# Gathering the third expert's rows right behind the second expert's, before the first scatter

## The chip, the core and the metric

The kernel runs on one core of a Trainium2 chip. The metric is the device time of one execution in microseconds (us). A profiled execution gives the trace, from which all single durations below come. The engines are named as in the profile: PE (matmuls), PEld (its weight loads), DVE, ACT, POOL and SP; SP and POOL mostly issue transfers.

## What is computed

The reference is an attention block whose output is the input of a mixture of experts:

```python
kv  = einsum('bhsd,bhse->bhde', k, v)           # batch 8, heads 8, seq 576, head_dim 64
out = einsum('bhsd,bhde->bhse', q, kv)
x   = out / sqrt(mean(out*out, -1) + 1e-6) * g_norm     # then reshaped to 4608 rows of 512

do_compute = x @ w_skip > 0                      # the other rows are returned as they are
e   = argmax(x @ w_gate)                         # one of 8 experts for each row
y   = softmax(x @ w_gate)[e] * (relu(x @ w1[e]) @ w2[e])   # w1: 512x1024, w2: 1024x512
out = x + y
```

## The kernel before

The attention part writes the rows of x to `out` in HBM and keeps the gate's logits. From these it works out, on the core, which rows go to which expert. The experts are sorted by their number of rows, so "expert 0" is the one with the most. Each has a fixed room for its rows (`ROOMS`: 352, 352, 320, 288, 288, 288, 256 and 256 rows, cut into pieces of 128, 64 and 32 rows by `PIECES`).

The rows of an expert are fetched from `out` with indirect DMAs issued by POOL, one for each piece (`gather_piece`, line L1084). They land in a tile `xg`; expert 0 has one of its own (`xg0`), the others share a pool of three (`gather_all`, L1376). PE transposes them (`expert_in`, L1093), layer 1 and layer 2 follow, DVE multiplies by the gate's value and adds x (`result`, L1336), and POOL scatters the rows back to `out` with an indirect DMA (L1339). Scatters are declared independent of each other, since each row has one slot. Gathers and scatters touch the same tensor `out`, so a gather behind a scatter in program order waits for its landing, and a scatter behind a gather likewise.

The order of instructions is written out by hand. Each engine takes its own in the order of the program text. In the stretch that matters here this is:

- Rows of expert 0 beyond the first 192, then those of expert 1, are gathered (L1500; six indirect DMAs on POOL, 134.9 to 142.4 us). The first 192 rows of expert 0 were gathered earlier (L863) and are already in the layers.
- Layer 2 for these first rows ends, layer 1 for the rest of expert 0 follows (L1112), and beside it the gate's values are placed (`first_tables`, L1405).
- The first 192 rows are scattered (`result` at L1407 and L1413, two indirect DMAs on POOL, at 154.07 and 155.40 us). Rows of expert 1 are transposed and its weight sums are begun on DVE (L1414).
- The rows of expert 2 are gathered (L1423, three indirect DMAs: two pieces of 128 rows and one of 64).
- Layer 2 for the rest of expert 0 (L1427, recorded at L1124): a piece of 128 rows, and one of 32 rows in matmuls with 32 columns, in two halves each. Then its results and scatters (L1430).
- Experts 1 to 7 follow, each in a form with 7 products in place of 8 (`fast_1`, `fast_2`; the matmuls are recorded at L1192, ACT's copies of partial sums at L1202, DVE's additions at L1196, its sums of weights at L1134 and L1140). At its beginning expert r gathers the rows of expert r + 2 (L1390).

The weights of an expert are 2 MB for each layer. SP loads them (L336 and L346) into two sets of tiles in turn, as soon as PE has read the set's former contents. The loads of expert 1 are issued at 142.0 and 142.7 us.

A second use of the same code, `experts(whole, ...)` at L1552, serves a loop that runs only when an expert has more rows than its room. It passes `yps0 = None`.

Of the kernel before, what the change touches and what calls it, by code (L numbers as in the profile page):

```python
# [17 lines left out]
def kernel(  # L18
# [213 lines left out]
    for a in range(2):  # L232
        r = slice(a * 64, (a + 1) * 64)
# [45 lines left out]
    for r, cap in enumerate(ROOMS):  # L279
        pieces, off = [], 0  # L280
# [710 lines left out]
    with tc.tile_pool(name="wpool_b", bufs=1, reuse_waits="tile") as wpool_b, \  # L991
# [89 lines left out]
        def gather_piece(xg, piece, src, asrc):  # L1081
            off, m, col, aside = piece
            idx = asrc if aside else src
            nc.gpsimd.indirect_dma_start(  # L1084
                out=x_of(xg, off, m), out_offset=None, in_=cut_rows(m)[:, :],
                in_offset=bass.IndirectOffsetOnAxis(ap=idx[:, col:col + 1], axis=0))

        def expert_in(xg, xt, piece):
            off, m = piece[0:2]
            x = x_of(xg, off, m)  # L1090
            xp = bank()[:, :].rearrange("p (j t) -> p j t", t=P)
            for j in range(DC * m // P):
                last = nc.tensor.transpose(out=xp[:, j, :], in_=x[:, j * P:(j + 1) * P],  # L1093
                                           identity=ident[:, :])
            turned(xt, xp, off, m)
            return last

        def new_xt():
            return ffn.tile([P, DC, CAP], FP32, tag="xt", name="xt")
# [8 lines left out]
        def layer_1(r, xt, ht, cols, fs):  # L1108
            for f in fs:
                hps = bank()  # L1110
                for dc in range(DC):
                    nc.tensor.matmul(out=hps[:, cols], lhsT=w_sb[r][0][:, dc, f * P:(f + 1) * P],  # L1112
                                     rhs=xt[:, dc, cols], start=(dc == 0), stop=(dc == DC - 1))
                nc.scalar.activation(out=ht[:, f, cols], in_=hps[:, cols], func=ACT.Relu)
# [69 lines left out]
        def do(work, n=None):  # L1184
            n = len(work) if n is None else min(n, len(work))
            for job in work[:n]:
                job()
            del work[:n]
# [141 lines left out]
        def result(piece, yps, xg, tables, group):  # L1330

            off, m, col, aside = piece
            n = DM * m // P
            rows, gate = tables[1 if aside else 0]
            x = x_of(xg, off, m)
            nc.vector.scalar_tensor_tensor(  # L1336
                out=x, in0=yps[:, 0:n], scalar=gate[:, col:col + 1], in1=x,
                op0=ALU.mult, op1=ALU.add)
            ins = nc.gpsimd.indirect_dma_start(  # L1339
                out=cut_rows(m)[:, :],  # L1340
                out_offset=bass.IndirectOffsetOnAxis(ap=rows[:, col:col + 1], axis=0),
                in_=x, in_offset=None, bounds_check=N * P // m - 1, oob_is_err=False)
            tc.declare_no_dep(ins.ins, group=group, reason="each row has one slot")
            tc.add_to_no_dep_group(group, ins.ins)
# [24 lines left out]
        def load_ahead(r, behind=None):  # L1369
            for ahead in (r, r + 1):  # L1370
                if ahead < E and ahead not in w_sb:
                    load_weights(ahead, wpool_b if ahead % 2 else wpool_a, behind)
# [3 lines left out]
        def gather_all(r, pieces, src, asrc):  # L1376
            if r < E:
                xgs[r] = xg0 if r == 0 else gather_pool.tile([P, CK, DM], FP32, tag="xg", name="xg",
                                                             bufs=3)
                for piece in pieces[r]:  # L1380
                    gather_piece(xgs[r], piece, src, asrc)

        def experts(pieces, widths, srcs, xt, ht, yps0, tables, group):

            for r in range(E):
                load_ahead(r)
                if yps0 is not None and r == E - 1:
                    nc.gpsimd.drain()
                if r:
                    gather_all(r + 2, pieces, *srcs)  # L1390
                todo = pieces[r]
                end = widths[r]
                new = {}

                def enter(some):
                    for piece in some:
                        expert_in(xgs[r + 1], new["xt"], piece)

                more = pieces[r + 1] if r + 1 < E else []
                if more:  # L1400
                    new["xt"] = new_xt()
                beside = []
                if r == 0:
                    if yps0 is not None:
                        tables = first_tables(lambda fs: layer_1(r, xt, ht, slice(KEPT, end), fs),  # L1405
                                              tables)
                        result(first[0], yps0[0], xgs[0], tables, group)  # L1407
                    else:
                        layer_1(r, xt, ht, slice(0, end), range(FC))
                    enter(more[0:1])  # L1410
                    if yps0 is not None:
                        tables = again_gates(tables)
                        result(first[1], yps0[1], xgs[0], tables, group)  # L1413
                    do(w1_sums(r + 1))  # L1414
                    enter(more[1:])
                else:
                    fast_1(r, xt, ht, end // 2, w2_sums(r), lambda: enter(more[0:1]))
                    enter(more[1:])
                if more:
                    n = widths[r + 1] // 2  # L1420
                    beside = x_sums(r + 1, new["xt"], n) + (w1_sums(r + 1) if r else [])
                if r == 0:
                    gather_all(2, pieces, *srcs)  # L1423
                    ys = [bank() for _ in todo]
                    for fs in (range(HF), range(HF, FC)):
                        for piece, y in zip(todo, ys):
                            layer_2(r, ht, piece, y, fs)  # L1427
                    do(beside, 4)
                    for piece, y in zip(todo, ys):
                        result(piece, y, xgs[r], tables, group)  # L1430
                    do(beside)
                else:
                    if yps0 is not None and r == 1:
                        rnd_i = rounds()
                    if yps0 is not None and r == E - 1:
                        n_rounds.append(nc.values_load(rnd_i[0:1, 0:1], min_val=1,
                                                       max_val=ROUNDS + 1))
                    of = {piece[0:2]: piece for piece in todo}
                    part = None
                    if yps0 is not None and r == 1:  # L1440
                        two = half_rows(tables[0][0])
                    if yps0 is not None and r == E - 1:
                        part = lambda c, half, y: half_result(c, half, y, xgs[r], two,
                                                              tables[0][1], group)
                    fast_2(r, ht, todo[2:], beside,
                           lambda key, y: result(of[key], y, xgs[r], tables, group), part)
                del w_sb[r]
                if more:
                    xt, ht = new["xt"], new_ht()
                    if yps0 is not None:  # L1450
                        blank(ht, r + 1)
# [45 lines left out]
        layer_2(0, ht_of, first[0], y, range(3, 4))  # L1497
        again_rows(arows, asrc, range(SOON, len(runs)))
        layer_2(0, ht_of, first[0], y, range(4, FC))
        for r in range(2):  # L1500
            gather_all(r, plan, src, asrc)
        gates()
        layer_2(0, ht_of, first[1], y_more, range(IN, 5))
# [2 lines left out]
        yps0 = [y, layer_2(0, ht_of, first[1], y_more, range(5, FC))]  # L1506
        load_ahead(0, landed)

        def first_tables(layer, tables):

            gp = g_ps[:, GB:GB + 3 * NCOL]
            half = NT // 2
            for i, t in enumerate((0, half)):
                bv = columns(t, half, colid_i, gate_k, 3, slot_pool, half)
                layer(range(i * FC // 2, (i + 1) * FC // 2))
                place(gp, bv, t, half, t == 0, t == half)
            gate = slot_gates_of(gp)
            return (tables[0], gate), (tables[1], None)

        def again_gates(tables):  # L1520
            agate = slot_pool.tile([P, NRES], FP32, tag="agate", name="agate")
            nc.vector.tensor_copy(out=agate[:, :], in_=again_of(tables[0][1], range(len(runs))))
            return tables[0], (tables[1][0], agate)
# [57 lines left out]
```

## Time and profile before

| | |
|---|---|
| median of three runs | 382.15 us (380.49 to 384.62) |
| profiled execution | 381.18 us, its span 379.4 us |
| instructions in the trace | 9624 |
| PE busy | 363.5 us |
| DVE busy | 244.9 us (65%) |
| ACT busy | 142.4 us (38%) |
| bytes moved by DMA | 81.70 MB, mean 215 GB/s |
| granted PE clock in the profiled execution | 0.997 |

A line of the order of time gives the start and the duration in us, the engine, the source line, the operation with its tiles (written to, then read from), and in brackets the idle time of the engine just before it and what ended it. "SPq" and "POOLq" are the queues of these engines. A stretch's row gives the busy time of PE, PEld, DVE, ACT and POOL in turn (with the number of instructions), then the granted clock, the busy share of the DMA engines and the GB/s that they moved. The ends of matmuls are modelled in the trace; when an engine that waits for a matmul starts is recorded.

### The profile page before, as it was taken

The page shows a single profiled execution, that of the slowest core. Times are in us where ns is not written, and L with a number is a line of the kernel's source. Part 1 is how long each engine was busy: PE and PEld are TensorE (multiplying, and loading weights), DVE is VectorE, ACT ScalarE, POOL GpSimd, SP SyncE. Part 2 cuts the span into 40 slices and gives each one's busy share as a digit, 9 for nine tenths or more (in the row PEclk, how much of TensorE's full clock was granted, in tenths as well). Part 3 has the DMA queues.
Part 4 walks back from the last instruction along what each step waited for, and adds up shares of the span by engine and source line. Part 5 has one row for each costly group of instructions (what it writes and reads, how often), then busy time and mean ns, then how long its engine had stood idle before and what let it go on. Part 6 is the DMA issues. An engine that isn't in the chain of part 4 may idle for free.

```text
span 379.4 us, 9624 instructions
## 1 busy us (share of the span) xinstructions
PE 363.5 (96%) x3848; PEld 312.1 (82%) x3848; DVE 244.9 (65%) x626; ACT 142.4 (38%) x383; POOL 124.9 (33%) x195
## 2 busy tenths in 40 slices
PE   8999999999988999989999999999999999999994
PEld 4688797898877759669879987988988988998983
DVE  3355457767878861846757656875876876877831
ACT  2466575766763302214402420430440430431410
POOL 7036467555677560234113303212202211202003
PEclk9999999999999999999999999999999999999998
DMA  8999999995669639945716362772662762700001
GB/s 288 394 391 387 402 402 400 404 372 196 189 242 262 184 98 323 387 145 199 250 39 218 127 224 59 244 269 51 235 226 70 263 197 95 269 3 28 29 1 53
DMA packets 32039, 81.70 MB, mean 215 GB/s; under 512 B 2474, under 2 KB 2482, under 8 KB 31988
## 3 DMA queue, kind: packets, MB, share of 16 engines
q1 hardware_dynamic: 28176, 69.47, 52.2%
q0 software_dynamic: 3792, 11.53, 9.1%
q8 instruction: 32, 0.52, 0.6%
q14 instruction: 19, 0.16, 0.1%
q10 hardware_dynamic: 20, 0.02, 0.1%
HBM read 66.80 MB, written 14.48 MB: 214 GB/s over the span
## 4 chain that ended last, share of the span: by engine, by line
PE 81%; issue 9%; ACT 3%; DVE 3%; POOL 2%; DMA 1%; POOLq 0%; DVEq 0%; ACTq 0%
PE bank L1192 44%; PE bank L1124 7%; PE o_ps L496 6%; PE sum_ps L379 5%; PE bank L1112 4%; PE q_ps L460 3%; PE g_ps L393 2%; PE bank L1093 2%; PE q_ps L170 2%; DMA xg<-out_dram,src 1%; DVE rs L518 1%; DVE xl L537 1%; ACT sq L510 1%; PE q_ps L814 1%; PE g_ps L411 1%
## 5 line engine op out<-in xcount | busy, mean ns | idle before, releaser
L1202 ACT COPY p<-bank 128x128 f32<-128x128 f32 (+6 forms) x70 | 20.8, 297 | 102.1 <-PE bank L1192 89.6
L1192 PE MATMUL bank<-xt,w 128*128 128x128 f32 (+5 forms) x336 | 55.5, 288 | 0.3 <-DVE bank L1196 0.3
L567 POOL TENSOR_TENSOR xb<-xl,g_b 128x512 f32<-128x512 f32 x36 | 44.4, 1235 | 32.3 <-DVE rs L532 30.4
L1192 PEld LDWEIGHTS bank<-xt,w 128*128 128x128 f32 x336 | 47.0, 190 | 2.2 <-DVE bank L1196 1.3
L1196 DVE TENSOR_TENSOR bank<-bank,p 128x128 f32<-128x128 f32 (+6 forms) x70 | 23.6, 337 | 37.1 <-PE bank L1192 35.5
L1192 PE MATMUL bank<-xs,s 128*128 128x128 f32 (+5 forms) x224 | 36.9, 289 | 1.6 <-ACT p L1202 1.6
L496 PE MATMUL o_ps<-kvd,qT 128*128 128x146 f32 x240 | 35.8, 290 | 1.0 <-ACT kvd L415 0.7
L1339 POOL DMA_INDIRECT out_dram<-xg,arows x9 | 10.6, 1174 | 74.4 <-DVE xg L1336 68.8
L1124 PE MATMUL bank<-w,ht 128*32 128x128 f32 (+2 forms) x436 | 34.5, 319 | 0.0
L518 DVE TENSOR_REDUCE rs<-sq 128x8 f32<-128x512 f32 x36 | 24.6, 682 | 15.1 <-ACT sq L510 14.9
L1192 PEld LDWEIGHTS bank<-xs,s 128*128 128x128 f32 x224 | 31.1, 190 | 2.7 <-ACT p L1202 2.6
L496 PEld LDWEIGHTS o_ps<-kvd,qT 128*128 128x128 f32 x240 | 31.6, 188 | 2.0 <-ACT kvd L415 1.5
L1339 POOL DMA_INDIRECT out_dram<-xg,rows x14 | 13.9, 994 | 55.6 <-DVE xg L1336 54.3
L1124 PEld LDWEIGHTS bank<-w,ht 128*32 128x32 f32 (+2 forms) x436 | 18.8, 120 | 13.2 <-issue 10.9
L537 DVE TENSOR_TENSOR xl<-o_ps,rs 128x584 f32<-128x584 f32 x34 | 26.1, 767 | 4.5 <-DVE rs L532 0.5
L1084 POOL DMA_INDIRECT xg<-out_dram,src x14 | 14.5, 1038 | 39.7 <-DMA out_dram<-xg,rows 13.4
L1192 PE MATMUL bank<-t,ht 128*128 128x256 f32 x112 | 27.1, 385 | 0.0
L1192 PE MATMUL bank<-w,ht 128*128 128x256 f32 x112 | 27.1, 384 | 0.0
L510 ACT ACTIVATE sq<-o_ps 128x512 f32<-128x512 f32 x34 | 20.3, 596 | 15.0 <-PE o_ps L496 14.4
L1192 PE MATMUL bank<-t,hs 128*128 128x256 f32 x112 | 25.3, 379 | 0.0
L379 PE MATMUL sum_ps<-v,k 64*64 64x64 f32 x1152 | 24.7, 223 | 0.4 <-issue 0.4
L379 PEld LDWEIGHTS sum_ps<-v,k 64*64 64x64 f32 x1152 | 20.8, 134 | 4.3 <-issue 1.9
(217 smaller groups left out, 679.5 us busy)
## 6 DMA issues: line engine op xcount, KB each, us to landing
w<-in_moe_w_dram SPq DMA_DIRECT2D x16, 2048.0 KB, 9.8
k<-in_k_dram SPq DMA_DIRECT2D x16, 576.0 KB, 9.9
v<-in_v_dram SPq DMA_DIRECT2D x16, 576.0 KB, 10.6
q<-in_q_dram SPq DMA_DIRECT2D x16, 576.0 KB, 11.2
out_dram<-xb SPq DMA_DIRECT2D x29, 256.0 KB, 8.9
out_dram<-xb POOLq DMA_DIRECT2D x7, 256.0 KB, 5.9
xg<-out_dram,src POOLq DMA_INDIRECT x16, 3.4
out_dram<-xg,rows POOLq DMA_INDIRECT x16, 6.9
```

The source lines that it names most:

```text
L379: nc.tensor.matmul(out=sum_ps[w * 64:(w + 1) * 64, a, u, :], lhsT=kt[r, 2 * u + w, c, :], rhs=vt[r, 2 * u + w, c, :], start=(c == 0), stop ...
L496: nc.tensor.matmul(out=ps[:, w, 0:2 * PK].rearrange("p (r k) -> p r k", r=2)[:, :, cols], lhsT=qT[:, w, a, :], rhs=kvds[b % KVD][:, u, w, ...
L510: nc.scalar.activation(out=sq[:, :, :, :], in_=heads(ps, G, G + 2 * D), func=ACT.Square)
L518: nc.vector.tensor_reduce(out=rs[:, :, :], in_=sq[:, :, :, :].rearrange("p x y (a d) -> p x (y a) d", a=2), axis=AX.X, op=ALU.add)
L537: nc.vector.tensor_tensor(out=xl[:, :, :, :].rearrange("p x y (a k) -> p x (y a) k", a=2), in0=ps[:, :, 0:2 * PK].rearrange("p x (h k) -> ...
L567: late.append((lambda: nc.gpsimd.tensor_tensor(out=xb[:, :, 4 * u * D:(4 * u + 4) * D].rearrange("p r (w x) -> p r w x", w=2), in0=xl[:, : ...
L1112: nc.tensor.matmul(out=hps[:, cols], lhsT=w_sb[r][0][:, dc, f * P:(f + 1) * P], rhs=xt[:, dc, cols], start=(dc == 0), stop=(dc == DC - 1))
L1124: nc.tensor.matmul(out=yps[q * m:(q + 1) * m, 0:n], lhsT=ht(f)[:, off:off + m], rhs=w_sb[r][1][:, f, q * n:(q + 1) * n], start=(f == 0), s ...
L1192: nc.tensor.matmul(out=out, lhsT=lhsT(i), rhs=rhs(i), start=start and i == 0, stop=i == k - 1, skip_group_check=True)
L1196: nc.vector.tensor_tensor(out=to, in0=x, in1=y, op=ALU.add)
L1202: nc.scalar.copy(out=t, in_=x)
L1339: ins = nc.gpsimd.indirect_dma_start(out=cut_rows(m)[:, :], out_offset=bass.IndirectOffsetOnAxis(ap=rows[:, col:col + 1], axis=0), in_=x, ...
```

## The change

The first loop of gathers takes in the third expert (r = 2), and the later call is left to the second use of the code, where `yps0` is `None`:

```diff
                 if r == 0:
-                    gather_all(2, pieces, *srcs)
+                    if yps0 is None:
+                        gather_all(2, pieces, *srcs)
                     ys = [bank() for _ in todo]
...
-        for r in range(2):
+        for r in range(3):
             gather_all(r, plan, src, asrc)
         gates()
```

On POOL the three indirect DMAs of expert 2 now stand behind the sixth gather and before the first two scatters. The tile that they fill is the third of the pool of three, as before. No other engine's instructions change in number or in order.

## The prediction

> **What bounds the kernel now.** I read the page first: the busy shares, then the chain that ended last. After that I read the order of time around the two places that the edit connects (137 to 148 us, where the gathers go, and 161 to 169 us, where they come from), and last the waits and the stretches of 5 us.
>
> ```profile
> PE 363.5 (96%) x3848; PEld 312.1 (82%) x3848; DVE 244.9 (65%) x626; ACT 142.4 (38%) x383; POOL 124.9 (33%) x195
> ...
> PE 81%; issue 9%; ACT 3%; DVE 3%; POOL 2%; DMA 1%; POOLq 0%; DVEq 0%; ACTq 0%
> ```
>
> The matmul engine carries 81% of the chain and is busy for 96% of the span. So a gather counts only where it makes PE wait. The third expert's rows are first read by PE (L1093) at 182.03. They are gathered here:
>
> ```profile
> 163.15 0.99 POOL L1084 DMA_INDIRECT xg<-out_dram,src  x1 [6.63 <-DMA out_dram<-xg,arows]
> 164.16 0.85 PE L1192 MATMUL bank<-xt,w 128*128 128x172 f32 x4
> 164.45 0.98 POOL L1084 DMA_INDIRECT xg<-out_dram,src  x1 [0.30 <-issue]
> 164.84 0.75 PE L1192 MATMUL bank<-xs,s 128*128 128x172 f32 x4
> 165.73 0.95 POOL L1084 DMA_INDIRECT xg<-out_dram,asrc  x1 [0.30 <-issue]
> 166.69 0.37 SPq L346 DMA_DIRECT2D w<-in_moe_w_dram  x1
> 166.70 0.35 DVE L1336 SCALAR_TENSOR_TENSOR xg<-bank,agate,xg 128x128 f32<-128x128 f32 x1 [2.69 <-PE bank L1192]
> 166.80 0.30 ACT L1202 COPY p<-bank 128x172 f32<-128x172 f32 x1 [10.92 <-issue]
> 167.16 0.85 PE L1192 MATMUL bank<-xs,s 128*128 128x172 f32 x4 [1.56 <-ACT p L1202]
> ```
>
> Two things are to be seen. First, POOL waited 6.63 us for a scatter's landing before the first of the three gathers, and nobody felt it: the last is issued by 166.68, and with the longest landing of any DMA on xg (7.2 us) it is there at 173.9, 8 us before PE reads it. The wait that the edit removes is hidden. Second, PE stands still for 1.56 us, and this is on the chain. The last matmuls of expert 0's layer 2 (L1124, 32 columns) are shown as ended by 164.2. Yet three engines that wait for PE all start together: SP at 166.69, DVE at 166.70, ACT at 166.80. The result really came about 2.5 us later than shown, and just when POOL's third gather ends (165.73 + 0.95 = 166.68). ACT's copy would else have run at 165.0, and PE's next product (167.16) at 165.6, when the one before it (164.84 + 0.75) is done.
>
> One more place looks like that, and it too has POOL issuing gathers beside PE instructions of fewer than 128 columns:
>
> ```profile
> 138.49 1.06 PEld L1124 LDWEIGHTS bank<-w,ht 128*64 128x64 f32 x12 [0.76 <-issue]
> 138.71 0.94 POOL L1084 DMA_INDIRECT xg<-out_dram,src  x1 [0.30 <-issue]
> 139.93 0.76 PE L1093 MATMUL bank<-ident,xg 128*128 128x128 f32 x5
> 139.95 1.19 POOL L1084 DMA_INDIRECT xg<-out_dram,asrc  x1 [0.30 <-issue]
> ...
> 141.44 0.94 POOL L1084 DMA_INDIRECT xg<-out_dram,asrc  x1 [0.30 <-issue]
> 141.98 0.58 ACT L828 COPY xt<-bank 128x512 f32<-128x512 f32 x1 [10.89 <-PE bank L1093]
> 142.00 0.37 SPq L336 DMA_DIRECT2D w<-in_moe_w_dram  x1
> ...
> 147.70 1.51 DVE L698 TENSOR_TENSOR bv<-ohc,gate_k 128x1296 bf16<-128x1296 bf16 x1 [6.74 <-PE g_ps L710]
> ```
>
> PE's transposes are shown as ended by 140.7, and ACT and SP, which wait for them, start at 141.98 and 142.00: 1.3 us late. Where POOL issues nothing, the same 32-column group costs no such delay (L1124 at 199.53 for 1.08 us, its DVE reader at 200.77). Where POOL gathers beside full 128-column products (178.06 to 181.76), these keep their step of 0.58 us:
>
> ```profile
> 178.93 0.75 PE L1192 MATMUL bank<-xt,w 128*128 128x172 f32 x4
> 179.51 0.75 PE L1192 MATMUL bank<-xs,w 128*128 128x172 f32 x4
> ```
>
> **The change part by part.**
>
> POOL's queue. Three DMA instructions (0.99 + 0.98 + 0.95 us, 0.3 us between) leave 163.15 to 166.68 and stand behind the gather that ends at 142.38. In the built program they wait for nothing that is late: lanes last used before 139 us and an old POOL write. So they issue at 142.7, 144.0 and 145.3 and end by 146.2. POOL's next work was at 154.07, behind 11.68 us of idle time; DVE idles from 141.0 to 147.70. Cost 0; cover 7.9 us.
>
> The scatters moved past. The first one (154.07) now waits for nine gathers in place of six, and behind it on POOL stand the second scatter, expert 0's other two scatters, a memset and the fourth expert's gathers. The third moved gather lands between 145.3 + 2.4 = 147.7 (the shortest landing on xg) and 145.3 + 6.9 = 152.2 (the scatters' landing in the traffic of 154 to 162 us, which it is nearest to). DVE has the scatter's data ready at 153.03 + 0.75 = 153.78. Cost 0, cover 1.6 us; without the cover still nothing until PE reads the fourth expert's rows at 217.58.
>
> The transfers. 320 rows of 2 KB are 0.655 MB, put beside the second expert's weights, where the DMA engines are full:
>
> ```profile
> 145.00:150.00 5.00, 5.00 (x55) 4.97 (x54) 1.54 (x2) 1.38 (x5) 0.00 (x0) 1.00 0.98 371
> 150.00:155.00 5.00, 4.77 (x57) 4.49 (x56) 1.90 (x7) 1.41 (x5) 0.93 (x1) 1.00 1.04 397
> ```
>
> At 397 GB/s (last column) they take 1.65 us from the weights. The first weight tile lands at 142.0 + 10.2 = 152.2 (issue, and the time to landing of this load), and DVE starts on it at 154.96, so 2.8 us of cover; then DVE's sums end at 161.69 and PE wants them at 164.16, another 2.5. Cost 0 up to a slip of 5.3 us.
>
> What goes. With no gather at 163.15 to 166.68, PE's 1.56 us there. Bounds: 0 if POOL is not the cause, 2.5 if the whole late completion counts. I take the 1.56 that the row of 167.16 shows as idle time. Next late is nothing new: at 165.6 PE has its operands, and SP's load of the third expert's second weights (166.69, first read by DVE at 203.97) only moves up. Expert 0's scatters can go at about 164.3, the fourth expert's gathers some us before 178.06, both far from PE's need. The new place costs PE from 0 to 2.5 us (the larger delay seen); I take 0, since layer 1 there (L1112, 142.78 to 147) uses 128 columns, and the nearest row is the 0.58 us step beside gathers at 178 us.
>
> A rule that speaks against this: the Trainium skill, "SBUF — State Buffer", section "SBUF: two separate sides", says that only VectorE and GpSimd share a port pair and that TensorE never waits for anyone. By it POOL's gathers cannot hold PE, the 1.56 us would stay, and the sum would be 0. The two late completions above, 1.3 and 2.5 us, look otherwise, so I go by the rows.
>
> Sum: 0 + 0 + 0 - 1.56. The profiled execution took 381.18 us with a span of 379.40, so 379.6. It lies 0.97 below the median of the three runs (382.15); from the median it is 380.6. I forecast 380.1, between them.
>
> **The rivals.**
>
> Nothing changes. PE's pause at 164 us has a cause of its own (the step from 32-column to 128-column work, or a loss that comes by chance), and the removed wait was hidden: 381.2 to 382.15. For it: only two such coincidences are in the trace. Against it: the 32-column groups at 199.53 and at 257.70 make the same step without a pause.
>
> The pause moves with the gathers. They hold layer 1 of expert 0 by up to 2.5 us in their new place while 1.56 us come back: 382.1 from the profiled run; 383.7 if the old pause stays as well. For it: every late completion has gathers near. Against it: the full-width products at 178 us.
>
> Slower: the second expert's weights come late. If the three gathers take turns with the weights for as long as three landings one after another (3 x 6.9 = 20.7 us, half of that time taken from the weights: 10.35), DVE's sums and with them PE are late by 10.35 - 5.3 = 5.1: 386.2. It decides from a slip of 5.3 us on. For it: an indirect DMA took 6.9 us in that traffic, twice its median of 3.4. Against it: 0.655 MB are 1.65 us.
>
> That the gathers are not ahead of the scatters after all is excluded by the built order.
>
> **How the numbers follow.** Forecast 0.55; nothing changes 0.22; the pause moves 0.12; weights late 0.07; unnamed 0.04. Three runs of before lie between 380.49 and 384.62, so I call 1% (3.8 us) what a measurement can tell from no change. The range goes from 378.0 (lowest run less 2.5) to 383.8 (the pause in both places), which leaves out the late weights and the unnamed. The forecast's own range is 378.9 (lowest run less 1.56) to 381. Faster by over 1% would need more than all of the pause: 0.04, from the unnamed and from chance. Slower by over 1%: 0.08, late weights and some of the unnamed. Within: 0.88.
>
> **What would show it.** Right: POOL's nine gathers follow one another from 134.9 to 146.2; SP's load, DVE's L1336 and ACT's L1202 start near 164.3 to 165.1 in place of 166.7; no idle time of 1.56 us before the third product; PE's L1093 for the third expert at about 180.5. Wrong, if L1112's eight ACT readers lose their step of 1.01 us, if DVE's first weight sum starts after 155, or if PE's pause at 164 is there without a gather beside it.

## The result, and the profile after

| | before | after |
|---|---|---|
| median, 22 runs each | 383.19 us (380.49 to 385.37) | 381.73 us (380.28 to 382.44) |
| ratio after / before, 95% interval | | 0.9962 [0.9947, 0.9978] |
| profiled execution, its span | 381.18 us, 379.4 | 381.81 us, 380.0 |
| row table (DVE L782) to the end of the span | 134.45 to 379.4: 244.9 us | 136.29 to 380.0: 243.7 us |

The change made the kernel 1.46 us faster in this comparison. The two profiled executions say the opposite by 0.6 us, and the last row of the table tells why: after reached the table of rows 1.84 us later, in a part of the program that the change does not touch (DVE's first reciprocal, L532, already starts at 21.14 against 19.58). From the table on, which is where the moved gathers stand, after needs 1.2 us less. So the two traces are compared from there, and 1.84 us are to be taken off a time of after to lay it beside one of before.

The page of after, busy shares and the chain that ended last:

```profile
PE 365.3 (96%) x3848; PEld 313.2 (82%) x3848; DVE 245.1 (64%) x626; ACT 142.3 (37%) x383; POOL 124.2 (33%) x195
...
PE 84%; issue 6%; DVE 3%; ACT 3%; POOL 2%; DMA 1%; POOLq 0%; DVEq 0%; ACTq 0%
```

PE carries 84% of the chain, 3 points more than before, and "issue" 3 points less. Idle time has gone and work has not. The waits of PE between 130 and 380 us (us in total, times, longest) say which, first in before:

```profile
PE bank L1192 <- ACT p L1202: 1.6, 1, 1.6
PE bank L1112 <- issue: 0.6, 1, 0.6
PE bank L1192 <- DVE bank L1196: 0.3, 1, 0.3
PE g_ps L1051 <- DVE gate L773: 0.2, 1, 0.2
```

and in after:

```profile
PE bank L1112 <- issue: 0.6, 1, 0.6
PE g_ps L710 <- issue: 0.5, 1, 0.5
PE g_ps L1051 <- DVE gate L773: 0.2, 1, 0.2
```

1.6 and 0.3 us are gone and 0.5 us have come: 1.4 us less, beside 1.2 us from the table to the end and 1.46 us between the medians; one execution of each cannot tell more closely. The 0.3 us are not the work of the moved gathers. They stand here in before, beside gathers for a later expert (two, from 302.76 to 305.03) that the change leaves where they are:

```profile
304.06 0.97 POOL L1084 DMA_INDIRECT xg<-out_dram,src  x1 [0.30 <-issue]
...
305.66 0.31 DVE L1196 TENSOR_TENSOR bank<-bank,u 128x136 f32<-128x136 f32 x1 [0.44 <-PE bank L1192]
...
306.02 0.73 PE L1192 MATMUL bank<-xt,w 128*128 128x136 f32 x4 [0.28 <-DVE bank L1196]
```

In after the same two gathers (303.37 to 305.72) cost PE no wait:

```profile
305.91 1.46 PE L1192 MATMUL bank<-xt,w 128*128 128x136 f32 x8
```

The order of time in after where the pause was (all lines are 1.84 us late against before):

```profile
165.79 0.75 DVE L1336 SCALAR_TENSOR_TENSOR xg<-bank,agate,xg 128x512 f32<-128x512 f32 x1 [1.55 <-PE bank L1124]
...
166.69 0.85 PE L1192 MATMUL bank<-xt,w 128*128 128x172 f32 x4
166.81 0.98 POOL L1339 DMA_INDIRECT out_dram<-xg,arows  x1 [7.13 <-DVE xg L1336]
166.82 0.37 SPq L346 DMA_DIRECT2D w<-in_moe_w_dram  x1
166.83 0.35 DVE L1336 SCALAR_TENSOR_TENSOR xg<-bank,agate,xg 128x128 f32<-128x128 f32 x1 [0.29 <-PE bank L1124]
...
167.38 1.45 PE L1192 MATMUL bank<-xs,s 128*128 128x172 f32 x8
167.62 0.30 ACT L1202 COPY p<-bank 128x172 f32<-128x172 f32 x1 [9.21 <-issue]
```

SP's load and DVE's second sum start 0.13 us after PE's first product of expert 1, where before they started 2.5 us after it (166.69 against 164.16), and PE's products follow one another (L1192 x8 without a bracket). The pause is gone from this place, and so are the gathers. Now the place that the gathers went to, first in before, when they were not there:

```profile
142.78 4.29 PE L1112 MATMUL bank<-xt,w 128*128 128x148 f32 x32 [0.64 <-issue]
144.09 0.29 ACT L1114 ACTIVATE ht<-bank 128x148 f32<-128x148 f32 x1 [1.36 <-PE bank L1112]
```

and in after:

```profile
143.78 0.58 ACT L828 COPY xt<-bank 128x512 f32<-128x512 f32 x1 [10.85 <-PE bank L1093]
...
144.53 0.94 POOL L1084 DMA_INDIRECT xg<-out_dram,src  x1 [0.30 <-issue]
144.58 4.29 PE L1112 MATMUL bank<-xt,w 128*128 128x148 f32 x32 [0.60 <-issue]
145.78 0.95 POOL L1084 DMA_INDIRECT xg<-out_dram,src  x1 [0.30 <-issue]
147.03 0.95 POOL L1084 DMA_INDIRECT xg<-out_dram,asrc  x1 [0.30 <-issue]
...
148.76 0.21 PE L710 MATMUL g_ps<-bv,oha_k 128*128 128x72 bf16 x1
149.46 0.73 PE L710 MATMUL g_ps<-bv,oha_k 128*128 128x72 bf16 x17 [0.49 <-issue]
149.52 0.67 ACT L1114 ACTIVATE ht<-bank 128x148 f32<-128x148 f32 x3 [4.99 <-PE bank L1112]
```

ACT reads the first result of L1112 4.94 us after that group began (149.52 - 144.58), in before 1.31 us after (144.09 - 142.78): 3.6 us later. Three results are then read at once (x3), so the step of 1.01 us between ACT's readers is lost, which the prediction named as a sign against it. PE stood still there for only 0.49 us, behind the first matmul of L710 and until just before the three results were read; the profile names nothing that it waited for. In the first comparison, then, the late completions moved along with the gathers, to a place where they cost less. What makes them is the question of the experiments.

### The profile page after: what moved, and what is told of

Same layout as the page of the kernel before. It is cut to its first block, busy times and chain, and to the rows that moved or that the text cites. A ratio compares the mean times of both kernels' runs of the same rounds, so it can differ in the third digit from the quotient of the medians.

```text
span 380.0 us, 9623 instructions
## 1 busy us (share of the span) xinstructions
PE 365.3 (96%) x3848; PEld 313.2 (82%) x3848; DVE 245.1 (64%) x626; ACT 142.3 (37%) x383; POOL 124.2 (33%) x195
## 4 chain that ended last, share of the span: by engine, by line
PE 84%; issue 6%; DVE 3%; ACT 3%; POOL 2%; DMA 1%; POOLq 0%; DVEq 0%; ACTq 0%
PE bank L1192 44%; PE bank L1124 9%; PE o_ps L496 6%; PE sum_ps L379 5%; PE bank L1112 4%; PE q_ps L460 3%; PE g_ps L393 2%; PE q_ps L170 2%; PE bank L1093 2%; DMA xg<-out_dram,src 1%; DVE rs L518 1%; DVE xl L537 1%; ACT sq L510 1%; PE q_ps L814 1%; PE g_ps L411 1%
## 5 line engine op out<-in xcount | busy, mean ns | idle before, releaser
L1192 PE MATMUL bank<-xt,w 128*128 128x128 f32 (+5 forms) x336 | 55.5, 288 | 0.1
L1192 PEld LDWEIGHTS bank<-xt,w 128*128 128x128 f32 x336 | 47.0, 190 | 2.0 <-DVE bank L1196 1.5
L1192 PE MATMUL bank<-xs,s 128*128 128x128 f32 (+5 forms) x224 | 36.7, 289 | 0.0
L1192 PEld LDWEIGHTS bank<-xs,s 128*128 128x128 f32 x224 | 31.1, 190 | 1.0 <-ACT p L1202 0.8
L1192 PE MATMUL bank<-t,ht 128*128 128x256 f32 x112 | 27.1, 385 | 0.0
L1192 PE MATMUL bank<-w,ht 128*128 128x256 f32 x112 | 27.1, 384 | 0.0
L379 PE MATMUL sum_ps<-v,k 64*64 64x64 f32 x1152 | 25.6, 228 | 0.6 <-issue 0.6
L379 PEld LDWEIGHTS sum_ps<-v,k 64*64 64x64 f32 x1152 | 21.7, 140 | 4.7 <-issue 2.1
L1192 PE MATMUL bank<-t,hs 128*128 128x256 f32 x112 | 25.3, 379 | 0.0
```

The costliest lines, as they stand in the source:

```text
L379: nc.tensor.matmul(out=sum_ps[w * 64:(w + 1) * 64, a, u, :], lhsT=kt[r, 2 * u + w, c, :], rhs=vt[r, 2 * u + w, c, :], start=(c == 0), stop ...
L1192: nc.tensor.matmul(out=out, lhsT=lhsT(i), rhs=rhs(i), start=start and i == 0, stop=i == k - 1, skip_group_check=True)
```

## The experiments

The expectations use letters for the theories. **A**: PE's results are seen late while POOL issues indirect DMAs, as the prediction has it. **B**: the transfers do it, whoever issues them. **C**: the pause is not tied to the gathers. After the first four runs came **D**: the late completions belong to the chip, or the session, of the first comparison. All runs below were made later, on three chips; which chip the first comparison ran on isn't recorded, nor whether all its runs were on one, so "there" and "then" cannot be told apart. Each ratio is against the kernel before on the same chip, and "the stage" is the time from the table of rows to the end of the span, which leaves out the uneven beginning (the table is ready at 134.1 to 138.0 us, whatever the kernel).

**Three plain loads at the old place.** The kernel before, with the third expert's gathers replaced by plain loads of the rows of the first slots, issued by ACT or by POOL. The third expert's rows are then not the right ones, and nothing else is changed.

```diff
+        def load_rows(r, pieces, queue):
+            xgs[r] = gather_pool.tile([P, CK, DM], FP32, tag="xg", name="xg", bufs=3)
+            for off, m, _, _ in pieces[r]:
+                queue.dma_start(out=x_of(xgs[r], off, m), in_=cut_rows(m)[0:P, :])
...
-                    gather_all(2, pieces, *srcs)
+                        load_rows(2, pieces, nc.scalar)
```

Issued by ACT:

> The kernel before, with the third expert's three gathers in their old place replaced by three plain loads of the same size, issued by ACT (rows 0 to 319 of out, so the third expert works on other rows than the reference). POOL then issues nothing between the second and the third scatter; the 0.655 MB still travel at the same time. Theory A (PE's completions come late while POOL issues indirect DMAs): no pause of PE at 164 us, SP's load and DVE's L1336 at most 0.3 us behind the last L1124, time 1.2 to 1.9 us below before. Theory B (the transfers themselves hold PE): the pause of 1.5 us stays, time within 0.4 us of before. Theory C (the pause is not tied to the gathers): the pause stays too.

Measured: 380.64 us, 1.0023 [1.0006, 1.0039]; stage 242.4 us. The interval just leaves out 1; 0.2 us of this stand in the stage.

With `nc.gpsimd` in place of `nc.scalar`:

> The kernel before, with the same three transfers in the old place as plain DMAs issued by POOL in place of indirect ones (rows 0 to 319 of out, so the third expert works on other rows than the reference). Theory A, if any DMA that POOL issues does it: the pause stays, time within 0.4 us of before. Theory A, if only the indirect form does it: no pause, 1.2 to 1.9 us below before. Theory B: the pause stays. Theory C: the pause stays.

Measured: 380.38 us, 1.0015 [0.9994, 1.0036]; stage 242.2 us. Neither trace has the pause, though in this one POOL issues there (order of time, POOL):

```profile
163.84 1.71 POOL L1386 DMA_DIRECT2D xg<-out_dram  x3 [6.52 <-DMA out_dram<-xg,arows]
```

This says little for A over B, because before itself took only 380.03 us on this chip (35 runs), 3.2 us less than in the first comparison. There was no pause left to explain.

**Gathers back at the old place.** The kernel after, and the fourth expert's three gathers where the third's had been:

```diff
-                if r:
+                if r > 1 or r == 1 and yps0 is None:
                     gather_all(r + 2, pieces, *srcs)
...
-                    if yps0 is None:
-                        gather_all(2, pieces, *srcs)
+                    gather_all(2 if yps0 is None else 3, pieces, *srcs)
```

> The changed kernel, with the fourth expert's three gathers moved from the start of expert 1 to the place from which the third expert's were taken (after the first two scatters). Theories A and B: the late completion is back at 164 to 168 us and with it PE's pause of about 1.5 us, time 1.2 to 1.9 us above the changed kernel, so 0.3 us below to 0.5 us above before. Theory C: the gain stays, 1.2 to 1.7 us below before.

Measured: 380.50 us, 1.0010 [0.9995, 1.0025]; stage 242.2 us. POOL's order of time:

```profile
167.53 0.99 POOL L1084 DMA_INDIRECT xg<-out_dram,src  x1 [6.34 <-DMA out_dram<-xg,arows]
168.82 0.97 POOL L1084 DMA_INDIRECT xg<-out_dram,src  x1 [0.30 <-issue]
170.10 1.47 POOL L1084 DMA_INDIRECT xg<-out_dram,asrc  x1 [0.30 <-issue]
```

The gathers are beside PE's first products of expert 1 once more, behind a wait of 6.34 us, and PE does not pause. Theory A did not expect that.

**Twelve gathers in a row.** The kernel after, with the fourth expert's rows in the first loop as well (`range(4)`, and the later call left out as in the diff above).

> The changed kernel, with the fourth expert's gathers ahead of all scatters too (twelve gathers in a row). Theories A and B: no pause at 164 us, but the completions of layer 1 (L1112) are late for some 7 us in place of 3.6, until ACT's late copies leave PE without a free bank: PE idle there 1 to 4 us, time 0 to 3 us above the changed kernel. Theory C: no change against the changed kernel, 1.2 to 1.7 us below before.

Measured: 380.43 us, 1.0013 [0.9999, 1.0028]; stage 242.2 us. Even the first scatter is late without a price: its data are ready at 152.69 (DVE L1336, 151.94 + 0.75), and it goes at 156.92.

**The two kernels of the study again, on a second chip.** No edit. This tells D from the others.

> The kernel before, unchanged, once more. Theory A (late completions of PE belong to the program: POOL's gathers at that place) gives a pause of about 1.5 us before the third product of expert 1 and 244.9 us from the row table (the last DVE instruction that writes src) to the end, as in the first profile. Theory D (they belong to the chip or the session, since the four variants of the last runs have none and take 242.2 to 242.4 us for that stretch wherever the gathers stand) gives no pause and 242.2 us where this chip has no late completions.

Measured: 380.17 us, 0.9991 [0.9976, 1.0006]; stage 242.2 us. The order of time at the place of the pause:

```profile
164.69 0.99 POOL L1084 DMA_INDIRECT xg<-out_dram,src  x1 [6.87 <-DMA out_dram<-xg,arows]
...
165.45 0.85 PE L1192 MATMUL bank<-xt,w 128*128 128x172 f32 x4
165.58 0.37 SPq L346 DMA_DIRECT2D w<-in_moe_w_dram  x1
165.59 0.35 DVE L1336 SCALAR_TENSOR_TENSOR xg<-bank,agate,xg 128x128 f32<-128x128 f32 x1 [0.29 <-PE bank L1124]
165.99 0.97 POOL L1084 DMA_INDIRECT xg<-out_dram,src  x1 [0.30 <-issue]
...
166.14 1.45 PE L1192 MATMUL bank<-xs,s 128*128 128x172 f32 x8
166.38 0.30 ACT L1202 COPY p<-bank 128x172 f32<-128x172 f32 x1 [9.21 <-issue]
...
167.26 0.95 POOL L1084 DMA_INDIRECT xg<-out_dram,asrc  x1 [0.30 <-issue]
```

and all that is left of PE's waits between 130 and 380 us:

```profile
PE g_ps L1051 <- DVE gate L773: 0.2, 1, 0.2
```

It is the same program as before, with the same wait on POOL (6.87 us) and the same gathers beside the same matmuls, and SP and DVE start 0.13 us after PE's first product in place of 2.5 us. The 1.6 us are not a property of the kernel.

> The changed kernel, unchanged, on the same chip as the run of the kernel before. Theory A: the ratio of the first comparison again, 0.9947 to 0.9978. Theory D on a chip without late completions: 0.999 to 1.002, and 242.2 us from the row table to the end in both; on a chip with them: the ratio of the first comparison.

Measured: 380.08 us, 0.9987 [0.9971, 1.0003]; stage 242.2 us. At the gathers' new place, ACT and POOL in the order of time:

```profile
143.57 0.29 ACT L1114 ACTIVATE ht<-bank 128x148 f32<-128x148 f32 x1 [2.00 <-PE bank L1112]
144.13 0.94 POOL L1084 DMA_INDIRECT xg<-out_dram,src  x1 [0.30 <-issue]
144.58 0.29 ACT L1114 ACTIVATE ht<-bank 128x148 f32<-128x148 f32 x1 [0.71 <-PE bank L1112]
145.38 0.95 POOL L1084 DMA_INDIRECT xg<-out_dram,asrc  x1 [0.31 <-issue]
145.58 0.29 ACT L1114 ACTIVATE ht<-bank 128x148 f32<-128x148 f32 x1 [0.71 <-PE bank L1112]
```

ACT's readers keep their step of 1.01 us right through the gathers. That goes against A and B at the new place too.

**Gathers held until PE's transposes.** The kernel after, with the second and third expert's gathers behind expert 0's transposes, so that none stands beside these (the new last argument of `gather_all` makes the first of them wait for the last transpose):

```diff
-        for r in range(3):
-            gather_all(r, plan, src, asrc)
+        gather_all(0, plan, src, asrc)
...
             landed = expert_in(xg0, xt0, piece)
+        for r in (1, 2):
+            gather_all(r, plan, src, asrc, landed if r == 1 else None)
```

> The changed kernel, with the gathers of the second and third expert held back until PE has transposed the rest of expert 0's rows, so that POOL issues nothing beside these transposes. Theory A: the late completion of the transposes (ACT's copy 1.3 us late, PE idle 0.6 us at 142 us) is gone, time 0.6 us below the changed kernel, unless layer 1 is held longer. Theory D on a chip without late completions: nothing to gain, within 0.3 us of the changed kernel.

Measured: 380.25 us, 0.9989 [0.9971, 1.0007]; stage 242.2 us. The gathers were issued from 142.58 up to 152.2 us (in after_again up to 146.3), which changed nothing either.

**A third chip, and the gathers put late.** Before, after, and a kernel that fetches the third expert's rows only as expert 1 begins:

```diff
+                if r == 1 and yps0 is not None:
+                    gather_all(2, pieces, *srcs)
                 if r:
                     gather_all(r + 2, pieces, *srcs)
...
-                if r == 0:
+                if r == 0 and yps0 is None:
                     gather_all(2, pieces, *srcs)
```

> The kernel before, unchanged, for a profile beside the next two on one more chip. Theory D: 242.2 us from the row table to the end where this chip has no late completions of PE, about 245 where it has. Theory A: about 245 in any case (already unlikely after the last runs).

Measured: 380.02 us (one run); stage 242.2 us.

> The changed kernel, unchanged, on one more chip. Theory D: if the profile of the kernel before shows 242.2 us, this one too, with a ratio of 0.998 to 1.002; if it shows late completions, about 1.2 us less than it, with a ratio of 0.994 to 0.998.

Measured: 380.12 us, 0.9995 [0.9977, 1.0013]; stage 242.2 us.

> The kernel before with the third expert's gathers still later: at the start of expert 1, behind expert 0's last two scatters and just ahead of the fourth expert's gathers. If the removed wait had the cover that the prediction gave it (8 us), the rows land 3 us or less before or after PE asks for them: time 0 to 1 us above before. If the old place was already on the edge, the whole delay of 8 to 10 us shows in the time.

Measured: 380.03 us, 0.9996 [0.9979, 1.0014]; stage 242.2 us. In its order of time POOL sends the three gathers here:

```profile
173.81 1.32 POOL L1084 DMA_INDIRECT xg<-out_dram,src  x1 [7.12 <-DMA out_dram<-xg,arows]
175.43 0.97 POOL L1084 DMA_INDIRECT xg<-out_dram,src  x1 [0.30 <-issue]
176.70 0.94 POOL L1084 DMA_INDIRECT xg<-out_dram,asrc  x1 [0.30 <-issue]
```

and PE reads them here, without idle time:

```profile
178.93 1.52 PE L1192 MATMUL bank<-xt,w 128*128 128x172 f32 x8
180.29 0.60 PE L1093 MATMUL bank<-ident,xg 128*128 128x128 f32 x4
```

So the third expert's rows can be gathered 10 us later than in before (164.69 in the execution above, less 1.33 us by which that one's table of rows was later, makes 163.36) and still no one feels it. That is about the end of the cover: the last gather lands 3.0 us after its issue at 176.70, and PE's first transpose of these rows starts at 180.29.

**The two kernels once more**, on a chip used above:

> The kernel before, unchanged, once more, to find out whether late completions of PE come back on another chip. Theory D (they belong to the chip or the hour of the first comparison): 242.2 us from the row table to the end and a time near 380.2 us on a chip like the last three; 244 to 246 us and a time near 383 us on a chip like the first.

Measured: 380.45 us, 1.0001 [0.9980, 1.0023]; stage 242.2 us.

> The changed kernel on the same chip. Theory D: the same time as before within 0.2% where the kernel before shows 242.2 us for the stretch; 0.2% to 0.5% less than before where it shows late completions.

Measured: 380.40 us, 1.0006 [0.9978, 1.0034]; stage 242.2 us. Like all runs since the first comparison it has no pause of PE in the stage but the 0.2 us at L1051.

What follows from the twelve: wherever the third expert's gathers stand (at 143, 164 or 174 us) and with the fourth's at 168, whichever engine issues the transfers, and with nine or twelve in a row, the stage takes 242.2 us (242.4 with ACT issuing). PE bounds it, with 0.2 us of waits. A (the prediction's reason) and B are refuted as properties of the program; C stands in the form of D. By it the first comparison is a stage of 242.2 us with 2.7 us (before) and 1.5 us (after) lost to late completions. Where these stand is seen by laying the first two executions beside before_again and after_again, each from its table of rows on. When layer 1 begins (L1112), before is at 8.33 us and after at 8.29, where before_again is at 7.63: both have lost 0.7 us beside the transposes. At the fourth product of expert 1, which starts at 167.84 in before and 167.43 in before_again, before has lost 2.4 us (33.39 against 30.98), so the old place cost 1.7. At the same product (168.66 and 165.61 us) after has lost 1.4 (32.37 against 30.99), so the new place cost 0.7. Before's other 0.3 us are those at 306.02. So the two places make 1.0 us of the difference between these executions.

The medians agree: 383.19 - 2.7 = 380.5 and 381.73 - 1.5 = 380.2, beside 380.0 to 380.5 for before in the later runs.

What made completions late in the first comparison, and why near gathers, stays open. It did not come back in any later run, so no experiment could be made on it, and D is shown only as far as it says that the other chips and hours are without it. That the gathers had a part in it is argued from one execution of each kernel, not shown: the same gathers stood beside late results in one and not in the other (306.02).

## Why the prediction was right and wrong

**The hidden wait: right.** The 6.63 us on POOL were worth nothing. The kernel that gathers at 173.81 shows it more strongly than the change does: 380.03 us and a stage of 242.2.

**POOL's queue: right.** The nine gathers ran from 136.70 to 147.98, that is 134.9 to 146.1 on before's clock (forecast 134.9 to 146.2).

**The scatters moved past: cost right, cover wrong.** The landing was put at up to 6.9 us after issue, and was 9.9 us for the second moved gather in after (8.3 to 8.9 us in after_again; after's trace has no landing for the third). The first scatter seems to have waited for it: in after its data were ready at 156.31 (155.56 + 0.75) and it went at 157.34, 1.0 us later, where before went 0.3 us after its data. In after_again it went 1.0 us after the last landing (145.38 + 8.3 = 153.7, and 154.67). The forecast's second line of defence held, that nobody needs the scatter soon: with twelve gathers the scatter was 4.2 us late, at no cost.

**The transfers: right.** They were to take 1.65 us from the weights; expert 1's first load took 12.3 us in after against 10.2 in before, and 12.3 against 11.0, 11.8 against 10.7 and 11.9 against 10.7 in the later pairs: 1.1 to 2.1 us. DVE's first weight sum started at 157.49, past the named sign of 155, but 1.84 us of that is the late beginning, and the 0.7 us that remain are not the weights': in after_again, where the load takes 12.3 us too, the sum starts 19.8 us after the table of rows (154.44 - 134.62), as in before_again (156.26 - 136.45).

**What goes, -1.56: the reason wrong, the size right in part by luck.** In the first comparison 1.46 us went. In the two executions this was 1.7 us at the old place (taken as 1.56), 0.7 us come back at the new one (taken as 0) and 0.3 us at 306.02 that the change does not touch. The step that failed is the one that took the two late completions for an effect of POOL's gathers on PE ("look otherwise, so I go by the rows"). In the later runs, on two chips, before has the same gathers beside the same matmuls and no pause, and the change brings nothing: 380.08 against 380.17, 380.12 against 380.02, 380.40 against 380.45 us, and 242.2 us for the stage in all six. There the rival "nothing changes", with "a loss that comes by chance", is what holds. The rule of the Trainium skill, "SBUF — State Buffer", section "SBUF: two separate sides", that TensorE waits for nobody at its port, agrees with these six runs. It speaks of SBUF's ports alone, so it does not say why results were late in the first comparison. The forecast weighed that rule against two coincidences in one execution and gave them the vote. "Only two such coincidences" was a misreading as well: the 0.28 us at 306.02 are a third, beside products of the full 128 columns, for which the new place had been put at 0. In the first comparison the rival "the pause moves with the gathers" was half true as well: layer 1's results came 3.6 us late, but cost 0.7 us in place of up to 2.5.

**The level: the term that made the time wrong.** 381.73 lies 1.63 us above the 380.1. Of this, 1.04 us is the starting point: the median of three runs was 382.15, that of 22 runs is 383.19. Another 0.49 us is the choice to go halfway from that median (380.6) to the profiled execution (379.6), "between them". Only 0.10 us is the sum itself (1.56 against 1.46). A profiled execution that is quick because of its beginning (its first reciprocal at 19.58 us, 1.56 us earlier than after's) says nothing about the median. The range of 378.0 to 383.8 held. Against the 383.19 of before the forecast would have been a gain of 3.1 us, over twice the 1.46 that came. The 1% (3.8 us) that the prediction took for the least that a measurement can tell was too coarse: with 22 runs each the interval is 0.8 to 2.0 us faster.

## What to carry to other kernels

A pause in one execution is a reason to look at a second execution, on another day or chip, before it is called a cost of the code: here the whole gain was a loss that the same program does not have in later runs. A transfer that is off PE's path can stand in many places for nothing (from 143 to 174 us here), and what shows this best is a kernel that moves it the wrong way. Compare two executions from an event that both share ahead of the change, and take the level from the median, not from the execution that happened to be profiled.

## What the runs showed of the hardware

- The spread between executions lies at the beginning. In the ten profiled executions of kernels with gathers in the later runs the table of rows is ready at 134.1 to 138.0 us, and the rest takes 242.19 to 242.23 us.
- A matmul's result can reach its readers late, by 3.6 us in after (4.94 against 1.31) and by 2.4 us in before (2.53 against 0.13 in before_again), without PE's records, the clock (0.999 and 0.997 granted) or the program showing a cause, in the first comparison and in none of the later runs. The modelled end of the matmul hides it; the start of the reader tells it.
- Beside 2 MB weight loads an indirect gather of up to 128 rows landed 8.3 to 9.9 us after its issue (the moved ones in after and after_again), where 3.0 to 3.6 us was the time for the first four of the same series (after_again).
